# A block of attention and a bilinear FFN: order of the work in the opening and in the first block's attention

## Chip, cores and metric

The kernel runs on one core of a Trainium2 chip. The metric is the device time of one execution in microseconds (us). The kernel before was timed in three runs, 2474.35, 2477.37 and 2477.96 us, with a median of 2477.37.

## What is computed

The input is x, 2048 rows of 576 numbers. The block has two halves, each with a normalisation ahead of it and a sum with its input behind it:

```python
h  = x + A(layernorm(x))
h2 = h + B(layernorm(h))
# A: 32 query heads of 18, one key head and one value head for all of them
q = (x @ wq) in heads; k = x @ wk; v = x @ wv
p = softmax(q k^T * 18**-0.5);  A = concat(p v) @ wo
# B: 4608 hidden units, no nonlinearity
B = ((x @ w_gate) * (x @ w_up)) @ w_down
```

All is float32. Nearly every product is made of three passes: an operand is split into a high part (type fp32r) and the remainder, and high x high, high x low and low x high are added up.

## The kernel before

**Blocks, groups, pairs.** The rows are cut into four blocks of 512 queries. Attention of a block goes by eight groups of four heads; a group goes over 16 key tiles of 128 keys. One call of `pair` (L482) makes the scores of two heads against one key tile: two matmuls (`scores`, L500, the two heads side by side on rows 0 to 63 and 64 to 127 of the array) into a PSUM tile `s` of two banks, and one exponential on ACT (L503) from it to an SBUF tile `P`. Two pairs make a key tile of a group. There are 2 x 16 x 8 = 256 pairs in a block and 1024 in all. `s` has two buffers, so a third pair's scores wait until the first one's exponential has been read.

**Values.** `values` (L505) multiplies the four heads' exponentials of one key tile with V, four column strips side by side, into the accumulator `acc`, which has one PSUM bank. `flush(n)` (L510) issues the values of the n oldest key tiles in the list `pend`. After a group's last tile DVE copies `acc` to `os` (L518), and the output's transposition and division follow later as an "aux" (`normalise`, L532, and `normal_heads`, L540), then the transposition of finished chunks (L572); `run_aux(1)` runs at most one of these a step.

**The other PSUM banks.** Eight banks: four for `s`, two with the tag `f`, one `m` (bounds, transposes of outputs), one `a` (accumulator; in the opening the key projection `psk`).

**The opening, `keys_values` (L141 to L317).** Before any attention, the four blocks of x are loaded, normalised (`stats` on DVE, `scale` on DVE or POOL, `apply` on ACT), transposed on PE (`turn`), and split into high and low on ACT and DVE (`parts`); then keys and values of the block are projected on PE (`project`, 14 passes into `psk`), and brought into the form of `kT` by ACT, DVE and POOL (`keys`, whose second half is the function it returns). The query weights wq come by five loads of 128 x 576 and are split by `split_wq`: the high part on ACT, the low part on POOL. The first seven heads' queries of block 0 are projected here too (the 14 `next(first)` and the one behind them), sent to memory, and read back head by head (`load_q`). A bound of each query's scores needs the largest absolute keys of all four blocks: `kab`, `psb`, `G`, then `bounds(0)` and `load_m`. After that the first scores can start. The order of the calls is the order on every engine (`manual_schedule`): each engine takes its instructions in the order in which the program issues them, and SP's DMA queue does too.

**The first block's attention.** The loop in `run` (L840 to L849) makes block 0's attention while the queries of the 19 remaining (block, seven heads) tiles are projected: `queries` (L320) is a generator that yields after each pass, a pass being two matmuls of 64 rows into the two banks `psq` and `psr` (tag `f`). Behind the 14th pass it issues the eviction on DVE (L344 to L349), the DMAs to `q_dram`, and goes on to the next tile, whose first pass needs the same two banks. One step of the loop is four pairs; after each of them `due` grows by RATE = 1.25 and passes are issued while it is over zero, each of which takes 1 off. At the end of the step come one aux and `flush(len(self.pend) - 1)`: the values of all key tiles but the newest, two as a rule. When the generator is at its end, `steps` (L796) goes on in the same steps of four pairs without passes: to the end of the group, where a flag decides whether a bound was too loose (`guard`), and to the end of block 0's pairs, with the projections of the outputs and weights of the FFN put between. Then `fill` and the FFN (`ffn`) place the other blocks' pairs among their own matmuls.

Of the kernel before, what the change touches and what calls it, by code (L numbers as in the profile page):

```python
# [14 lines left out]
F32 = mybir.dt.float32  # L15
# [7 lines left out]
P = 128  # L23
# [32 lines left out]
class Block:  # L56
# [84 lines left out]
    def keys_values(self):  # L141
# [7 lines left out]
        xs = x01 + [x23[:, 0], x23[:, 1]]  # L149
        wqr = [(self.qp if c < 2 else self.qb).tile([P, D], F32, tag="q" if c < 2 else "qs", name=f"wqr{c}")  # L150
               for c in range(4)]
        for b in range(NB):
            for s in range(NQ):
                sp.dma_start(xs[b][:, s, :], self.x[b * TB + s * P: b * TB + (s + 1) * P, :])
            if b == 0:
                sp.dma_start(self.C, self.cst)
                sp.dma_start(wkv, self.wkv)
            if b == 1:
                for c in range(4):
                    sp.dma_start(wqr[c], self.wq[:, c, :])  # L160
        w_h = self.pp.tile([P, 5, P], F32R, tag="P", name="w_h")
# [60 lines left out]
        def project(b):  # L222
            psk = psks[b] = self.ps_a(f"psk{b}")
            for i, (w, m) in enumerate(passes(w_h, w_l, self.XT[b])):
                pe.matmul(psk, w, m, start=(i == 0), stop=(i == 13))
# [7 lines left out]
        def keys(b):  # L233

            sl = slice(b * TB, (b + 1) * TB)
            kk = self.pp.tile([P, 2, TB], F32R, tag="P", name=f"kk{b}")
            hi, k2 = kk[0:64, 0], f32(kk[0:64, 1])
            act.activation(hi, psks[b][0:64], AF.Identity, bias=nmean[0:64])
            dve.tensor_reduce(kabs[0:64, b:b + 1], f32(hi), AX.X, ALU.max, apply_absolute_value=True)

            def rest():
                if b:
                    dve.tensor_copy(kv[:, sl], psks[b])
                del psks[b]
                pool.tensor_scalar(k2, kv[0:64, sl], mb, nmb[0:64], ALU.mult, ALU.add)
                dve.scalar_tensor_tensor(self.kT[0:64, sl], f32(hi), ma, k2, ALU.mult, ALU.add)
                sp.dma_start(f32(self.kT[64:120, sl]), f32(self.kT[0:56, sl]))
            return rest

        first = self.queries(0)  # L250

        def split_wq(c):
            act.copy(self.wq_h[:, c], wqr[c])
            pool.tensor_tensor(self.wq_l[:, c], wqr[c], f32(self.wq_h[:, c]), ALU.subtract)

        act.copy(w_h, wkv)
        pool.tensor_tensor(w_l, wkv, f32(w_h), ALU.subtract)
        stats(0, 4)
        scale(0, 4, dve)
# [3 lines left out]
        scale(4, 8, pool)  # L263
        turn(0)
        stats(8, 12)
        scale(8, 12, pool)
        parts()
        split_wq(0)
        split_wq(1)
        apply(1)  # L270
        wqr.append(self.qp.tile([P, D], F32, tag="q", name="wqr4"))
        sp.dma_start(wqr[4], self.wq[:, 4, :])
        stats(12, 13)
        twice(dve)
        turn(1)
        stats(13, 16)
        scale(12, 16, pool)
        project(0)
        parts()
        apply(2)  # L280
        twice(dve)
        mean()
        turn(2)
        project(1)
        parts()
        keys(0)()
        split_wq(2)
        apply(3)
        twice(pool)
        late = keys(1)  # L290
        split_wq(3)
        split_wq(4)
        turn(3)
        late()
        project(2)
        parts()
        for _ in range(14):
            next(first)
        next(first)
        q = self.qt[0, 0] = self.qp.tile([P, 2, TB], F32R, tag="q", name="q0_0")  # L300
        self.load_q(q, 0, 0)
        keys(2)()
        project(3)
# [7 lines left out]
        self.load_m(q, 0, 0)  # L311
        late()
        psv = self.ps_a("psv")
        for t in range(NT):
# [5 lines left out]
    def queries(self, b):  # L320

        pe, act, dve, sp = self.pe, self.act, self.dve, self.sp
        for i, (h0, n) in enumerate(QT):
# [9 lines left out]
            else:  # L333

                psr = self.ps_f(f"psr{b}_{i}")
                for k, (w, m) in enumerate(passes(w_h, w_l, self.XT[b])):
                    for o, ps in ((0, psq), (64, psr)):
                        pe.matmul(ps[:r], w[o:o + 64], m[o:o + 64], start=(k == 0), stop=(k == 13))
                    yield 1
                    if k == 5 and self.tqs and self.tqs[0][0] < max(b, 1):  # L340
# [12 lines left out]
            self.tqs.append((b, h0, n, tq))  # L353
            if b == i == 0:
                yield 0
        if b == NB - 1:
            yield STEP
            yield STEP
            self.bounds(b)
# [436 lines left out]
    def steps(self, on):  # L796

        while on():
            for i in range(4):
                self.pair()  # L800
            self.run_aux(1)
            self.flush(len(self.pend) - 1)

    def run(self):
# [9 lines left out]
        with ExitStack() as st:  # L814
# [11 lines left out]
            with tc.tile_pool(name="p0q", bufs=1) as self.p0q:  # L826
# [3 lines left out]
                with tc.tile_pool(name="qb", bufs=2) as self.qb:  # L830
# [9 lines left out]
                    while live:  # L840
                        for i in range(4):
                            self.pair()
                            due += RATE
                            while due > 0 and live:
                                z = next(others, None)
                                live = z is not None
                                due -= z or 0
                        self.run_aux(1)
# [35 lines left out]

STEP = 2
RATE = 1.25
P_BUFS = 6
# [94 lines left out]
```

## Time and profile before

| What | Before |
|---|---|
| median of three runs | 2477.37 us |
| the profiled execution | 2473.66 us |
| its span, first to last instruction | 2471.9 us |
| first scores, PE L502 | 65.69 us |
| PE busy, share of the span | 2379.9 us, 96% |
| ACT busy | 1233.9 us, 50% |
| DVE busy | 1000.1 us, 40% |
| POOL busy | 356.4 us, 14% |
| exponentials, ACT L503 | 1024, 1027 ns each |

The profile is of one execution. Its page has the span in 40 slices, with the busy share of each engine as a digit (9 is 90% or more) and the clock granted to PE as a digit too. A row of the timeline gives the start in us, the length in us, the engine, the line, the operation, output and input, and how many instructions of that kind follow each other; in brackets stands how long the engine stood idle ahead of it and what ended that. A row of the waits gives who waited (engine, tile, line), for whom, the us in total, the number of times and the longest. A row of a group gives the instructions' count, their busy time and mean length in ns, and the idle time ahead of them. PEld is the loading of weights into PE. A matmul's length includes its way through the array, so that rows overlap; the time from start to start is what PE spends on it.

### The profile page before, as it was taken

What the parts mean: (1) busy time and instruction counts of PE and PEld (TensorE: products, weight loads), DVE (VectorE), ACT (ScalarE), POOL (GpSimd) and SP (SyncE); (2) the same over time, 40 slices, a digit from 0 to 9 for tenths busy, and PEclk for the clock granted to TensorE, in tenths of its full rate; (3) what the DMA queues carried; (4) which work ended last, traced back from release to release, by engine and by line L of the source; (5) the groups of instructions that cost most, each with busy time, mean ns of one, the idle gap of its engine ahead of it and who ended that gap; (6) DMA issues with size and microseconds to landing.
All of it is one profiled execution on the core that took longest, in us unless ns stands there. A gap on an engine that the chain in (4) does not pass through costs nothing. (4 is left out here: it accounts for less than half of the span.)

```text
span 2471.9 us, 44165 instructions
## 1 busy us (share of the span) xinstructions
PE 2379.9 (96%) x18833; PEld 1669.0 (68%) x18833; DVE 1000.1 (40%) x1719; ACT 1233.9 (50%) x1385; POOL 356.4 (14%) x402
## 2 busy tenths in 40 slices
PE   5888888999999999999999999999999999999999
PEld 4333333467776777776777767677767778888888
DVE  6322222433343334433333335343433364545544
ACT  5666665666556555466556564555565511111110
POOL 4000000011111111111111111111111112222221
PEclk8899997999999999999999999999999999999999
DMA  3211112222122221332212121241221122432221
GB/s 134 76 54 56 60 48 90 62 75 69 58 76 66 66 69 63 92 112 73 68 61 75 66 71 51 76 147 45 75 75 57 64 77 87 140 106 92 97 97 58
DMA packets 68706, 190.54 MB, mean 77 GB/s; under 512 B 7736, under 2 KB 7864, under 8 KB 68504
## 3 DMA queue, kind: packets, MB, share of 16 engines
q1 hardware_dynamic: 68504, 187.66, 23.8%
q8 instruction: 149, 2.44, 0.4%
q14 instruction: 53, 0.43, 0.1%
HBM read 159.39 MB, written 19.40 MB: 72 GB/s over the span
## 5 line engine op out<-in xcount | busy, mean ns | idle before, releaser
L503 ACT ACTIVATE P<-s 128x1024 f32<-128x1024 f32 x1024 | 1031.9, 1027 | 742.2 <-PE s L502 626.3
L743 PE MATMUL pg<-X,ws 64*128 64x512 f32 x2565 | 706.1, 392 | 0.0
L743 PE MATMUL pu<-X,ws 64*128 64x512 f32 x2565 | 705.6, 392 | 0.0
L743 PEld LDWEIGHTS pg<-X,ws 64*128 64x128 f32 x2565 | 474.4, 186 | 64.8 <-issue 6.1
L743 PEld LDWEIGHTS pu<-X,ws 64*128 64x128 f32 x2565 | 474.0, 186 | 40.0
L507 PE MATMUL acc<-P,V 128*32 128x512 f32 x4096 | 485.8, 605 | 5.8 <-DVE os L518 5.1
L502 PE MATMUL s<-q,kT 56*128 56x512 f32 x2048 | 442.6, 426 | 34.6 <-ACT P L503 28.2
L716 PE MATMUL y<-wds,ha 128*128 128x288 f32 x2304 | 464.1, 296 | 2.5 <-ACT ha L85 1.2
L716 PEld LDWEIGHTS y<-wds,ha 128*128 128x128 f32 x2304 | 368.4, 188 | 27.8 <-issue 25.2
L502 PEld LDWEIGHTS s<-q,kT 56*128 56x128 f32 x2048 | 196.4, 186 | 220.1 <-ACT P L503 108.6
L716 PE MATMUL y<-wds,hl 128*128 128x288 f32 x1152 | 340.1, 295 | 0.1
L743 PE MATMUL gu<-X,ws 64*128 64x512 f32 x2646 | 307.3, 389 | 0.0
L85 POOL CAST ws<-wr 128x1152 fp32r<-128x1152 f32 x144 | 166.3, 1155 | 970.0 <-PE pu L743 405.0
L507 PEld LDWEIGHTS acc<-P,V 128*32 128x32 f32 x4096 | 120.8, 110 | 273.1 <-issue 255.4
L743 PEld LDWEIGHTS gu<-X,ws 64*128 64x128 f32 x2646 | 247.8, 185 | 54.8 <-issue 4.2
L762 DVE TENSOR_TENSOR hf<-pu,g 128x512 f32<-128x512 f32 x95 | 65.7, 692 | 526.4 <-ACT g L758 526.4
L718 DVE TENSOR_TENSOR h<-h,y 128x288 f32<-128x288 f32 x384 | 172.8, 454 | 252.9 <-PE y L716 252.7
L758 ACT COPY g<-gu 128x512 f32<-128x512 f32 x49 | 28.8, 587 | 376.2 <-PE gu L743 376.2
L85 POOL CAST wds<-wdr 128x576 fp32r<-128x576 f32 x144 | 146.4, 1036 | 485.6 <-PE y L716 479.7
L716 PEld LDWEIGHTS y<-wds,hl 128*128 128x128 f32 x1152 | 216.1, 188 | 0.4 <-DVE hl L86 0.4
L86 DVE TENSOR_TENSOR ws<-wr,ws 128x1152 fp32r<-128x1152 f32 x144 | 204.5, 1420 | 0.0
L86 DVE TENSOR_TENSOR hl<-hf,ha 128x512 fp32r<-128x512 f32 x144 | 101.0, 702 | 152.6 <-ACT ha L85 152.6
(143 smaller groups left out, 1327.6 us busy)
## 6 DMA issues: line engine op xcount, KB each, us to landing
wr<-in_wgu_dram SPq DMA_DIRECT2D x144, 576.0 KB
wdr<-in_wd_dram SPq DMA_DIRECT2D x144, 288.0 KB
q<-q_dram SPq DMA_DIRECT2D x64, 216.0 KB
q_dram<-qs SPq DMA_DIRECT2D x16, 504.0 KB
X<-X SPq DMA_DIRECT2D x28, 256.0 KB
x<-in_x_dram SPq DMA_DIRECT2D x16, 288.0 KB
h<-in_x_dram SPq DMA_DIRECT2D x16, 288.0 KB
out_dram<-h SPq DMA_DIRECT2D x16, 288.0 KB
```

The lines of the kernel that those rows point to most:

```text
L85: (copy or self.cast)(hi, src)
L86: self.dve.tensor_tensor(lo, src, f32(hi), ALU.subtract)
L502: self.pe.matmul(s_[:, i], self.kT[o:o + 56, t * P:(t + 1) * P], q[o:o + 56, pr], start=True, stop=True)
L503: self.act.activation(p_, s_, AF.Exp, scale=SCALE)
L507: self.pe.matmul(acc[32 * j:32 * j + 32, :], self.V[:, t, :], Ps[j // 2][:, j % 2, :], start=(t == 0), stop=(t == NT - 1), skip_group_chec ...
L716: pe.matmul(y[:, :HD], m, w, start=(i == 0), stop=(i == len(ms) - 1))
L718: dve.tensor_tensor(hs, hs, y[:, :HD], ALU.add)
L743: pe.matmul(ps, w[o:o + 64, wk, c], X[o:o + 64, xk, c], start=(j == 0), stop=(j == 26))
L758: act.copy(g, pg)
L762: dve.tensor_tensor(hf, pu, g, ALU.mult)
```

## The change

It changes only order and sizes of work, not what is computed.

In the first attention a step has two pairs instead of four. RATE is 3.0 and is added once a step, after the first of the two pairs; passes follow there, the second pair follows without any. `flush(len(self.pend) - 1)` then issues one key tile's values. A tile's last pass takes 4 from `due` instead of 1, and `bounds(3)` at the end of the last block comes after one yield of 4 instead of two of 2. `steps` too has two pairs a step.

In the opening, the first seven heads' columns of wq come as one load of 128 x 5 x 126, behind the weights of keys and values and ahead of the second block's x; ACT and POOL split them directly after those weights. The other heads' columns come as one load of 128 x 5 x 450, issued behind the second block's keys, into the buffer that held the third and fourth block of x; POOL alone makes their high and low parts, tile by tile, at the end of the opening. `psk` uses the bank `a` for blocks 0 and 2 and a bank `f` for blocks 1 and 3. The tiles `kk` come from the ring of two buffers `qs` instead of the six of `P`. The first queries' passes stand ahead of the third block's normalisation, the projection of block 0 ahead of the second block's, and statistics, key steps and loads are ordered anew:

```diff
-        wqr = [(self.qp if c < 2 else self.qb).tile([P, D], F32, ...) for c in range(4)]
+        wqr = self.qp.tile([P, 5, 7 * DH], F32, tag="q", name="wqr0")
...
-            if b == 1:
-                for c in range(4):
-                    sp.dma_start(wqr[c], self.wq[:, c, :])
+                sp.dma_start(wqr, self.wq[:, :, 0:7 * DH])
...
-            psk = psks[b] = self.ps_a(f"psk{b}")
+            psk = psks[b] = (self.ps_f if b % 2 else self.ps_a)(f"psk{b}")
...
-            kk = self.pp.tile([P, 2, TB], F32R, tag="P", name=f"kk{b}")
+            kk = self.qb.tile([P, 2, TB], F32R, tag="qs", name=f"kk{b}")
...
+        w = (slice(None), slice(None), slice(0, 7 * DH))
+        act.copy(self.wq_h[w], wqr)
+        pool.tensor_tensor(self.wq_l[w], wqr, f32(self.wq_h[w]), ALU.subtract)
         stats(0, 4)
...
         turn(0)
+        parts()
         stats(8, 12)
         scale(8, 12, pool)
-        parts()
-        split_wq(0)
-        split_wq(1)
+        project(0)
         apply(1)
-        wqr.append(self.qp.tile([P, D], F32, tag="q", name="wqr4"))
-        sp.dma_start(wqr[4], self.wq[:, 4, :])
         stats(12, 13)
         twice(dve)
         turn(1)
-        stats(13, 16)
+        stats(13, 15)
+        for _ in range(14):
+            next(first)
+        parts()
+        stats(15, 16)
         scale(12, 16, pool)
-        project(0)
-        parts()
+        mean()
         apply(2)
         twice(dve)
-        mean()
         turn(2)
-        project(1)
-        parts()
-        keys(0)()
-        split_wq(2)
-        apply(3)
-        twice(pool)
-        late = keys(1)
-        split_wq(3)
-        split_wq(4)
-        turn(3)
-        late()
-        project(2)
-        parts()
-        for _ in range(14):
-            next(first)
         next(first)
         q = self.qt[0, 0] = self.qp.tile([P, 2, TB], F32R, tag="q", name="q0_0")
         self.load_q(q, 0, 0)
+        project(1)
+        parts()
+        late = keys(0)
+        apply(3)
+        twice(pool)
+        late()
+        turn(3)
+        project(2)
+        late = keys(1)
+        parts()
+        late()
+        wqr = self.otp.tile([P, 5, D - 7 * DH], F32, tag="oT", name="wqr1")
+        sp.dma_start(wqr, self.wq[:, :, 7 * DH:])
         keys(2)()
         project(3)
         late = keys(3)
...
         late()
+        for h0, n in QT[1:]:
+            w, o = (slice(None), slice(None), slice(h0 * DH, (h0 + n) * DH)), 7 * DH
+            pool.tensor_copy(self.wq_h[w], wqr[:, :, h0 * DH - o:(h0 + n) * DH - o])
+            pool.tensor_tensor(self.wq_l[w], wqr[:, :, h0 * DH - o:(h0 + n) * DH - o], f32(self.wq_h[w]), ALU.subtract)
...
-                    yield 1
+                    if k < 13:
+                        yield 1
...
-            if b == i == 0:
-                yield 0
+            yield 0 if b == i == 0 else 4
         if b == NB - 1:
-            yield STEP
-            yield STEP
+            yield 4
             self.bounds(b)
...
         while on():
-            for i in range(4):
-                self.pair()
+            self.pair()
+            self.pair()
             self.run_aux(1)
             self.flush(len(self.pend) - 1)
...
                     while live:
-                        for i in range(4):
-                            self.pair()
-                            due += RATE
-                            while due > 0 and live:
-                                z = next(others, None)
-                                live = z is not None
-                                due -= z or 0
+                        self.pair()
+                        due += RATE
+                        while due > 0 and live:
+                            z = next(others, None)
+                            live = z is not None
+                            due -= z or 0
+                        self.pair()
                         self.run_aux(1)
                         self.flush(len(self.pend) - 1)
...
-STEP = 2
-RATE = 1.25
+RATE = 3.0
```

More of the change, by code (lines that the diff above doesn't have):

```diff
@@ L149, in keys_values @@
         xs = x01 + [x23[:, 0], x23[:, 1]]
-        wqr = [(self.qp if c < 2 else self.qb).tile([P, D], F32, tag="q" if c < 2 else "qs", name=f"wqr{c}")
-               for c in range(4)]
+        wqr = self.qp.tile([P, 5, 7 * DH], F32, tag="q", name="wqr0")
         for b in range(NB):
@@ L250, in keys_values @@
         first = self.queries(0)
-        def split_wq(c):
-            act.copy(self.wq_h[:, c], wqr[c])
-            pool.tensor_tensor(self.wq_l[:, c], wqr[c], f32(self.wq_h[:, c]), ALU.subtract)
         act.copy(w_h, wkv)
         pool.tensor_tensor(w_l, wkv, f32(w_h), ALU.subtract)
+        w = (slice(None), slice(None), slice(0, 7 * DH))
+        act.copy(self.wq_h[w], wqr)
+        pool.tensor_tensor(self.wq_l[w], wqr, f32(self.wq_h[w]), ALU.subtract)
         stats(0, 4)
```

## The prediction

> **What bounds the kernel now.** The page first: span and slices. The profiled execution took 2473.66 us, its span 2471.9.
>
> ```profile
> span 2471.9 us, 44165 instructions
> PE   5888888999999999999999999999999999999999
> PEclk8899997999999999999999999999999999999999
> ```
>
> A slice is 61.8 us. From slice 7 on PE is hardly ever idle, and the change moves nothing after that slice: of 1024 pairs (a pair is two heads' scores against one key tile) the two kernels order all after the 278th alike. It touches slices 0 to 7; in 1 to 6 PE is eight tenths busy. The engine beside it there is ACT; the waits and its group from 75 to 345 us show both.
>
> ```profile
> ACT P L503 <- PE s L502: 89.4, 60, 4.1
> PEld s L502 <- ACT P L503: 76.1, 106, 0.9
> PEld acc L507 <- DVE os L518: 10.4, 6, 1.8
> PEld psq L338 <- DVE qs L344: 9.9, 14, 1.3
> PEld psr L338 <- DVE qs L345: 7.7, 14, 0.6
> L503 ACT ACTIVATE P<-s 128x1024 f32<-128x1024 f32 x189 | 179.8, 1028 | 89.4 <-PE s L502 89.4
> ```
>
> ACT is busy 179.8 of the 270 us. Neither engine is full, so they wait for each other: exponentials wait for scores (60 times, about once a step of four pairs), and scores wait for exponentials, because there are two score banks. One clean step in the timeline shows the loop:
>
> ```profile
> 151.08 0.50 PE L502 MATMUL s<-q,kT 56*128 56x512 f32 x2
> 151.69 3.77 ACT L503 ACTIVATE P<-s 128x1024 f32<-128x1024 f32 x4 [1.35 <-PE s L502]
> 151.88 0.40 PE L502 MATMUL s<-q,kT 56*128 56x512 f32 x2
> 152.11 0.40 PE L338 MATMUL psr<-XT,wq_h 64*126 64x512 f32 x1
> 152.76 0.50 PE L502 MATMUL s<-q,kT 56*128 56x512 f32 x2 [0.25 <-ACT P L503]
> 153.68 0.50 PE L502 MATMUL s<-q,kT 56*128 56x512 f32 x2 [0.19 <-ACT P L503]
> 154.34 1.92 PE L507 MATMUL acc<-P,V 128*32 128x512 f32 x16
> 156.20 0.50 PE L502 MATMUL s<-q,kT 56*128 56x512 f32 x2
> ```
>
> The step takes 156.20 - 151.08 = 5.12 us. ACT works 3.77 of it and then stands 1.35: PE puts both key tiles' values (1.86, from 154.34) in one block at the end, when ACT has only two scores in hand. Earlier in the step PE stands for a bank. A score or a query pass costs PE 0.23 (151.88 to 152.11).
>
> **The steps after the change.** A step is two pairs: a score, up to three passes, a score, one key tile's values. What one tile's block costs alone shows further on, in the fill before the FFN:
>
> ```profile
> 416.26 0.49 PE L502 MATMUL s<-q,kT 56*128 56x512 f32 x2
> 416.69 1.06 PE L507 MATMUL acc<-P,V 128*32 128x512 f32 x8
> 417.69 0.49 PE L502 MATMUL s<-q,kT 56*128 56x512 f32 x2
> 418.11 1.06 PE L507 MATMUL acc<-P,V 128*32 128x512 f32 x8
> ```
>
> From score to score 417.69 - 416.26 = 1.43: the score, the block, and two changes between them. It is dearer than half of a double block (1.00 against 0.93), and that is in the sum. A new step adds a score and n passes at 0.235 each: 2.37 for n = 3, 2.13 for 2, 1.90 for 1, 1.66 for 0. ACT needs 3.77/2 = 1.89 for two pairs, so a step is the larger of the two. It fits: an exponential starts 0.61 after its score (151.08 to 151.69) and its bank is free some 1.6 after it, before the same bank is asked for at 2.37; the values use the tile before, done 0.3 into the step. I see no wait in a clean step, and PE becomes the bound.
>
> The pull on the query generator: a step gives 3, a pass takes 1, and the last of a tile's 14 takes 4, so a tile takes 17. Three tiles go through 17 steps as 3 3 3 3 2, 1 3 3 3 3 1, 2 3 3 3 3 0: twelve of 2.37, two of 2.13, two of 1.90, one of 1.89, together 38.4 (42 passes). The 19 tiles left for this stage and the end of the last one make 110 steps (220 pairs, as before: 55 steps of four): six such rounds 230.4, then four of 2.37, one of 2.13 and three empty 17.3: **247.7 us**.
>
> Beside it on PE, moved but equal in number: the bounds' matmuls, transposes of the outputs and of the chunks.
>
> ```profile
> 354.68 0.66 PE L545 MATMUL pt<-C,os 128*128 128x128 f32 x4
> 373.22 1.36 PE L367 MATMUL psg<-tq,G 126*32 126x512 f32 x5
> ```
>
> Three groups of 1.36, four single ones at a fifth of that, nine transposes at 0.66: 11.1. The waits on DVE: at a tile's end the next pass now comes a score, a block and a score later, some 1.9 us after the last; DVE freed the second bank 1.9 after it before:
>
> ```profile
> 158.25 0.40 PE L338 MATMUL psr<-XT,wq_l 64*126 64x512 f32 x1
> 159.42 0.69 DVE L345 TENSOR_TENSOR qs<-psq,qs 126x512 f32<-126x512 f32 x1
> 160.16 0.50 PE L338 MATMUL psr<-XT,wq_h 64*126 64x512 f32 x1 [0.23 <-DVE qs L345]
> ```
>
> So it is met, just. The accumulator's bank likewise: a whole step now stands between one group's last block and the next group's first. Of the 28 us of such waits in the quoted rows I leave 4, for chunk transposes that follow the outputs' a step later, when DVE may be late, and 1.6 for the first step, whose PE work ran below full clock before and will again. Sum 264.4. Before:
>
> ```profile
> 65.69 1.01 PE L502 MATMUL s<-q,kT 56*128 56x512 f32 x2 [0.20 <-DMA q<-m_dram]
> 378.59 0.74 PE L502 MATMUL s<-q,kT 56*128 56x512 f32 x4
> ```
>
> 378.59 - 65.69 = 312.9 (pairs 1 to 220). **Gain 48.5.** Bounds: ACT alone would need 220 x 0.943 = 207, so not over 106; with every such wait kept (28 in 270 us, 32 in all), 28 more, a gain of 20.5.
>
> **The opening.** It ends with the key bound, which needs the last key projection. That one waited for its bank:
>
> ```profile
> 34.36 2.41 ACT L189 ACTIVATE xh<-x,n,ya 128x576 f32<-128x576 f32 x3
> ...
> 40.71 2.82 POOL L254 TENSOR_TENSOR wq_l<-wqr,wq_h 128x576 fp32r<-128x576 f32 x2 [2.44 <-ACT wq_h L253]
> 44.32 0.74 DVE L246 SCALAR_TENSOR_TENSOR kT<-kk,C 64x512 fp32r<-64x512 f32 x1 [2.82 <-POOL kk L245]
> 44.99 2.34 DVE L86 TENSOR_TENSOR XT<-tr,XT 128x1024 fp32r<-128x1024 f32 x2
> 47.36 0.69 DVE L95 TENSOR_TENSOR XT<-trt,XT 64x512 fp32r<-64x512 f32 x1
> 51.70 1.19 PE L225 MATMUL psk<-XT,w_h 128*128 128x512 f32 x2 [3.28 <-DVE kvw L243]
> 57.87 0.68 ACT L238 ACTIVATE kk<-psk,nmean 64x512 fp32r<-64x512 f32 x1 [8.25 <-PE psk L225]
> ```
>
> Its input was ready at 48.05 (47.36 + 0.69), it began at 51.70: with two banks 3.65 go. What then is late is DVE, which has the third tile's keys to copy first (one copy at 0.69): 0.7 back. DVE also stood 2.82 at L246, behind POOL's two weight splits; these leave, and the input is ready earlier.
>
> Against that stands the last tile's normalisation. Its statistics now come behind the second tile's splits on DVE (2.34 + 0.69 = 3.0), while POOL, which makes the scale of them, loses two weight splits ahead of it (2.82, priced as the two above). And the first weights' split has a price of its own:
>
> ```profile
> 9.46 1.53 POOL L257 TENSOR_TENSOR w_l<-kvw,w_h 128x640 fp32r<-128x640 f32 x1 [8.04 <-ACT w_h L256]
> 9.51 1.50 DVE L116 TENSOR_TENSOR ta<-ya 128x4 f32<-128x4 f32 x1
> ```
>
> A DVE instruction on four columns took 1.50 beside POOL's subtraction, to its end. A second subtraction, of 630 columns, now follows it beside the same chain: up to 1.5 later. The normalisation began at 34.36; it comes between 0 and 4.5 later, and stringing these durations queue by queue I get 2.7 (37.1). DVE's 2.82 less the part that this uses up leaves the input some 2 earlier. Last, the clock:
>
> ```profile
> 50.00:60.00 10.00, 6.42 (x16) 4.75 (x16) 3.15 (x7) 0.68 (x1) 0.77 (x1) 0.66 0.42 133
> ```
>
> The projection ran at a granted clock of 0.66 (the column before the DMA share), from 51.70 to just before 57.87, where 14 passes at 0.235 take 3.3. It began after 3.28 us of idle PE and will now follow the third one closely; I take 2 for it. Sum 3.65 - 0.7 + 2 + 2: **gain 7**, at least 1 (clock and POOL gains lost, the split late), at most 11. If the low clock came with the moment and not after idling, the gain is 5.
>
> The Trainium skill says in "TensorE: Matmul & The Clock Gate", section "Part 1: The HAM clock gate (the "warmup" mystery)", that an idle window of about 3.4 us halves the clock and a busy one restores it. By that rule the projection runs at full clock, as in my sum; the trace agrees in so far as 0.66 follows 3.28 us of idling.
>
> The strip of weights that ACT and POOL split before the first normalisation has rows of 126 x 4 = 504 bytes. The Trainium skill, "DMA: Bandwidth & Descriptors", section "Specifications", puts full rate at 512 bytes and more, with a read-modify-write below. By that page the strip is late. No row shows such a load; the nearest is the weights of keys and values, issued at 3.05 and used at 8.65:
>
> ```profile
> 3.05 0.43 SPq L157 DMA_DIRECT2D kvw<-in_wkv_dram  x1
> 8.65 0.73 ACT L256 CAST w_h<-kvw 128x640 fp32r<-128x640 f32 x1 [6.65 <-DMA kvw<-in_wkv_dram]
> ```
>
> At that rate the strip, issued at 3.5, lands by 9.5 and costs nothing; at twice the time it lands near 14.7, holds ACT's queue with the first normalisation behind it, and takes 1 to 2 us back. I take the first.
>
> POOL's eight splits of the other weights start when its last key step is done. The first piece must be there by the third pass: at most 1 us late. Their load, now a late one, stands in SP's queue behind the second tile's keys, some 6 us ahead of the bound's small DMAs.
>
> From pair 221 to 278 steps of two help only where outputs aren't projected: gain 1 (0 to 4; the flag's wait is untouched).
>
> **Sum**: 48.5 + 7 + 1 = 56.5, hence 2473.7 - 56.5 = 2417.2 for an execution like the profiled one. The median of the three runs shown, 2477.4, is 3.7 above it, so the median comes to 2420.9; I say **2420**.
>
> **Rivals.**
> 1. DVE's waits stay: a tile's five evictions, the bounds and the outputs share DVE, and "met, just" fails each time. For it: 0.2 us of margin. Against it: five at 0.69 or less are 3.5 of a tile's 13 us. 14 to 28 more: 2434 to 2448.
> 2. PE's parts pack better than the rows say and ACT's 207 us is the bound: 264.4 falls to some 225, 2381. Against it: the 1.43 stands in the rows.
> 3. The opening does not shorten: the strip late, the splits in the way, the clock low: 2427.
> 4. Slower. PE busier in the first attention lowers the clock it is granted there, as it did between 50 and 60 us. PE's 264 us turn into 400 at 0.66: 136 lost against 57 won, 2556. It decides at a mean of 264/321 = 0.82. Against it: the slices from 9 on have PE full at a clock of nine tenths and more.
>
> **How the numbers follow.** Forecast (gains 45 to 70, 2407 to 2432) 0.74; rival 1 0.12; rival 2 0.04; rival 3 0.07; rival 4 0.03. 2404 to 2440 takes in the forecast, the third and most of the first, and leaves out about 0.15. A measurement here tells 0.2%, 5 us, from no change: faster 0.96, same 0.01, slower 0.03.
>
> **What would show it.** ACT's idle, a third of the time from 75 to 345 us, falls to a fifth; exponentials come in twos, 2.4 apart; L338's waits for L344 and L345 nearly vanish; the first score stands near 58.7, the 221st pair's near 323; from the FFN on nothing differs but the start. It is wrong if passes or blocks cost more behind each other than in the rows quoted, or if a wait in each step, for a bank or for DVE, shows up instead.

## The result, and the profile after

The kernel after took 2412.61 us (median of four runs, 2410.95 to 2415.04), the kernel before 2475.86 (four runs, 2472.33 to 2477.96). The ratio is 0.9747, with a 95% interval of 0.973 to 0.9764. The forecast was 2420, the range 2404 to 2440. The profiled execution took 2414.04 us; before it was 2473.66, so 59.6 less, and 56.5 had been forecast. By the medians it is 63.3 less; the forecast of 2420 lay 57 below the median of three known then.

The page after, span, PE and PE's granted clock in 40 slices:

```profile
span 2412.3 us, 44160 instructions
...
PE   5999989999999999999999999999999999999999
...
PEclk9999999999999999999999999999999999999999
```

Slices 1 to 4 and 6 have gone from 8 to 9; the one 8 left, slice 5, holds the wait for the flag. To see where the 59.6 us came from, I cut each span at three rows of the timeline: the first score, the 221st pair, and the first transposition for the FFN (`tx`). The first two rows of the kernel after:

```profile
59.65 1.07 PE L498 MATMUL s<-q,kT 56*128 56x512 f32 x2 [1.48 <-DMA q<-m_dram]
...
325.07 0.73 PE L498 MATMUL s<-q,kT 56*128 56x512 f32 x4
```

| Stage (us) | Before | After | Gain | Forecast |
|---|---|---|---|---|
| opening, to the first score | 65.7 | 59.65 | 6.0 | 7 |
| pairs 1 to 220 | 312.9 | 265.4 | 47.5 | 48.5 |
| 221st pair to `tx` (472.84, 412.23) | 94.3 | 87.2 | 7.1 | 1 |
| from `tx` to the end | 1999.1 | 2000.1 | -1.0 | 0 |

**The first attention.** The waits of the kernel after between 70 and 312 us (who waited, for whom, us in total, times, longest), and its group of exponentials from the same stretch:

```profile
PEld s L498 <- ACT P L499: 77.7, 95, 0.9
ACT P L499 <- PE s L498: 45.4, 92, 2.3
```

```profile
L499 ACT ACTIVATE P<-s 128x1024 f32<-128x1024 f32 x202 | 196.8, 1024 | 46.0 <-PE s L498 45.4
```

ACT stands 46.0 of 242 us, a fifth instead of a third, and now about once in two exponentials, 0.5 us at a time. Waits on DVE for the query banks are gone from PE. The 77.7 us in the first row are no loss: it is the weight load that stands there, ahead of its turn. What the matmuls themselves waited for, from 80 to 300 us, is four rows before and two after:

```profile
PE s L502 <- ACT P L503: 13.5, 57, 0.5
PE acc L507 <- DVE os L518: 4.2, 5, 0.9
PE psq L338 <- DVE qs L344: 4.0, 6, 0.8
PE psr L338 <- DVE qs L345: 2.9, 12, 0.3
```

```profile
PE to L134 <- DVE ob L550: 2.0, 1, 2.0
PE acc L503 <- DVE os L514: 2.0, 1, 2.0
```

One clean step in the timeline, from score to score 69.65 - 67.30 = 2.35 us, with nothing in brackets on PE:

```profile
67.30 0.50 PE L498 MATMUL s<-q,kT 56*128 56x512 f32 x2
...
67.90 1.95 ACT L499 ACTIVATE P<-s 128x1024 f32<-128x1024 f32 x2 [0.47 <-PE s L498]
...
68.33 0.39 PE L498 MATMUL s<-q,kT 56*128 56x512 f32 x2
68.66 1.06 PE L503 MATMUL acc<-P,V 128*32 128x512 f32 x8
69.65 0.50 PE L498 MATMUL s<-q,kT 56*128 56x512 f32 x2
```

**The opening** of the kernel after, in the rows that answer to those of the prediction:

```profile
8.96 1.51 DVE L117 TENSOR_TENSOR ta<-ta,va 128x4 f32<-128x4 f32 x1
9.09 0.72 ACT L252 CAST wq_h<-wqr 128x630 fp32r<-128x630 f32 x1 [0.25 <-DMA wqr<-in_wq_dram]
10.41 1.43 POOL L253 TENSOR_TENSOR wq_l<-wqr,wq_h 128x630 fp32r<-128x630 f32 x1
10.51 1.35 DVE L122 SCALAR_TENSOR_TENSOR ya<-ta,yia 128x4 f32<-128x4 f32 x1
...
12.09 0.16 DVE L117 TENSOR_TENSOR ta<-ta,va 128x4 f32<-128x4 f32 x1
...
38.31 3.14 ACT L186 ACTIVATE xh<-x,n,ya 128x576 f32<-128x576 f32 x4 [1.73 <-POOL n L178]
...
46.33 0.50 PE L222 MATMUL psk<-XT,w_h 128*128 128x512 f32 x1 [0.23 <-DVE XT L86]
...
49.72 0.68 ACT L235 ACTIVATE kk<-psk,nmean 64x512 fp32r<-64x512 f32 x1 [3.08 <-PE psk L222]
...
51.53 0.74 DVE L243 SCALAR_TENSOR_TENSOR kT<-kk,C 64x512 fp32r<-64x512 f32 x1 [0.97 <-POOL kk L242]
52.20 0.67 DVE L236 TENSOR_REDUCE kabs<-kk 64x1 f32<-64x512 f32 x1
```

The last key projection waits for no bank: it starts at 46.33 (51.70 before), as soon as the first pieces of its input are there, and is done in 3.39 us (6.17 before). Then DVE keeps the fourth tile's keys waiting: ready at 50.40, they are taken up at 52.20. Before, DVE took them up 0.72 after ACT began on them (57.87):

```profile
58.59 0.68 DVE L239 TENSOR_REDUCE kabs<-kk 64x1 f32<-64x512 f32 x1 [5.39 <-ACT kk L238]
```

### The profile page after: what moved, and what is told of

Read it like the earlier page. It is cut to its first block, busy times and chain, and to the rows that moved or that the text cites. A ratio compares the mean times of both kernels' runs of the same rounds, so it can differ in the third digit from the quotient of the medians.

```text
span 2412.3 us, 44160 instructions
## 1 busy us (share of the span) xinstructions
PE 2357.6 (98%) x18833; PEld 1658.7 (69%) x18833; DVE 999.1 (41%) x1719; ACT 1235.2 (51%) x1381; POOL 357.9 (15%) x406
## 4 chain that ended last, share of the span: by engine, by line
PE 95%; DVE 2%; ACT 1%; issue 1%; DMA 1%; POOL 0%; SPq 0%; ACTq 0%; POOLq 0%; DVEq 0%
PE acc L503 19%; PE y L712 19%; PE pg L739 14%; PE gu L739 12%; PE s L498 12%; PE pu L739 11%; PE yo L608 3%; PE psq L335 2%; PE pt L541 1%; ACT P L499 1%; PE to L134 0%; PE tx L657 0%; DVE bsa L100 0%; PE psr L335 0%; DVE XT L86 0%
## 5 line engine op out<-in xcount | busy, mean ns | idle before, releaser
L503 PE MATMUL acc<-P,V 128*32 128x512 f32 x4096 | 491.2, 599 | 2.6 <-DVE os L514 2.0
L498 PE MATMUL s<-q,kT 56*128 56x512 f32 x2048 | 434.0, 421 | 12.9 <-DVEq L388 8.0
L503 PEld LDWEIGHTS acc<-P,V 128*32 128x32 f32 x4096 | 114.4, 109 | 250.4 <-issue 225.1
L758 DVE TENSOR_TENSOR hf<-pu,g 128x512 f32<-128x512 f32 x95 | 65.7, 691 | 528.6 <-ACT g L754 528.6
```

Source lines behind the costliest of these rows:

```text
L498: self.pe.matmul(s_[:, i], self.kT[o:o + 56, t * P:(t + 1) * P], q[o:o + 56, pr], start=True, stop=True)
L503: self.pe.matmul(acc[32 * j:32 * j + 32, :], self.V[:, t, :], Ps[j // 2][:, j % 2, :], start=(t == 0), stop=(t == NT - 1), skip_group_chec ...
L758: dve.tensor_tensor(hf, pu, g, ALU.mult)
```

## The experiments

Times are medians. Where a ratio to the kernel before stands beside one, it has its 95% interval; one with no ratio is a single run. Stages are cut as above, in the one execution of each kernel that was profiled.

| Kernel | Time | First score | Pairs 1 to 220 | To `tx` | After `tx` |
|---|---|---|---|---|---|
| loop_only | 2417.68 | 64.9 | 264.6 | 87.4 | 1996.9 |
| opening_only | 2465.79 | 59.9 | 313.0 | 91.1 | 1999.1 |
| values_by_two | 2440.23 | 59.4 | 293.4 | 87.2 | 1998.0 |
| double_score | 2435.53 | 58.7 | 287.8 | 87.2 | 2000.0 |
| short_exp | 2449.25 | 66.0 | 287.3 | 93.8 | 2000.4 |
| steps_four | 2421.16 | 59.6 | 265.0 | 91.7 | 1998.9 |
| one_bank | 2422.0 | 69.4 | 264.6 | 87.3 | 1999.0 |
| split_later | 2411.03 | 57.8 | 265.0 | 87.1 | 1997.2 |
| keys_behind | 2411.22 | 55.8 | 266.3 | 87.0 | 2000.4 |

In values_only and no_off the flag comes at another pair, so for those two only the sum of the two middle stages compares.

### The two halves of the change

loop_only is the kernel before with the loop, `steps` and the generator's yields of the kernel after. opening_only is the kernel after with those taken from before:

```diff
-                        self.pair()
-                        due += RATE
+                        for i in range(4):
+                            self.pair()
+                            due += RATE
...
-RATE = 3.0
+STEP = 2
+RATE = 1.25
```

> The opening of the kernel before with the loop and the later steps of the changed one. Stages of the profiles so far: first score at 65.69 us before and 59.65 after; 220 pairs from there in 312.9 and 265.4; from the 221st pair to the transposes ahead of the FFN 94.3 and 87.2. If the stages don't act on each other, this kernel has 65.7, 265 and 87: 6 us more than the changed kernel, about 2419. Rival: the low clock of the opening's end is carried into the loop and the loop needs the new opening for its gain: 270 or more in the second stage.

> The opening of the changed kernel with the loop and the later steps of the one before. If the stages don't act on each other: first score at 59.7, then 313, then 94: 6 us less than the kernel before, about 2470. Rival: part of the loop's gain comes from the opening (weights at hand, a warmer clock): under 308 in the second stage.

loop_only took 2417.68 us, 0.9765 (0.9749 to 0.9782), opening_only 2465.79, 0.9957 (0.9941 to 0.9974). In the first two stages the halves add up: the loop alone turns 312.9 us into 264.6, the opening alone 65.7 into 59.9, and neither moves the other's stage by a microsecond. So the loop's gain isn't the opening's, and nearly nine tenths of what these two stages gain (47.5 of 53.5) belong to it. The whole times do not add up as well: by the medians of their session the halves gain 59.6 and 11.5 us, together 71.1 where both gave 63.3, and opening_only came out 4 us below the 2470 expected. Some 3 of that is the stage up to `tx`, where opening_only gained 3.2 with the order of the kernel before; why is not shown.

### What in the loop makes it faster

values_only keeps values at each key tile, but places the passes as before, one or two behind each pair, with no step off at a tile's end. values_by_two keeps steps of two and three passes, but issues values every other step, for two key tiles. no_off lets a tile's last pass take 1 from `due`, so that the next tile's first pass may follow at once. Their edits, in this order and cut to the lines that matter:

```diff
-                        self.pair()
-                        due += RATE
-                        while due > 0 and live:
...
-                        self.pair()
+                        for i in range(2):
+                            self.pair()
+                            due += RATE
+                            while due > 0 and live:
```

```diff
-                        self.flush(len(self.pend) - 1)
+                        if self.n_pair % 4 == 0:
+                            self.flush(len(self.pend) - 1)
```

```diff
-                    if k < 13:
-                        yield 1
+                    yield 1
...
-            yield 0 if b == i == 0 else 4
+            if b == i == 0:
+                yield 0
```

> The changed kernel, but query passes are issued as before: RATE 1.25 after each of the two pairs, no step off at a tile's end. Values stay at each key tile. My theory of the prediction (values at each tile take PE and ACT apart, PE becomes the bound): second stage 265 plus the waits for DVE at tiles' ends, 10 to 25, so 275 to 290. Rival, that three passes between a step's scores make the gain: 295 or more.

> The changed kernel with the values of two key tiles every second step; passes stay at three a step with a step off. My theory of the prediction taken strictly (the double block of values is what starves ACT) says that much of the gain goes: second stage 285 or more. The rival worked out by rows: a score, three passes, a score twice, then the double block is 1.04 + 0.24 + a wait of 0.4 for the bank + 1.04 + 0.33 + 1.86 = 4.9 for four pairs, against 4.74 in the changed kernel: only 5 to 10 us more, 270 to 276, since the three passes between the scores already hide the exponentials.

> The changed kernel, but a tile's last pass takes 1 like the others, so that the next tile's first pass may follow it in the same step. If the step off is what removed the waits for DVE's evictions: they come back in two tiles of three, some 1.7 us each, and 3 us for more steps without passes: second stage 285 to 290 instead of 265. Rival, that PE has other work to do by then in any case: 265 to 270.

values_only took 2427.44 us, 0.9799 (0.9783 to 0.9815); its two middle stages take 368.3 us against 352.6 of the kernel after, 15.7 more. values_by_two took 2440.23, 0.9854 (0.9838 to 0.9871), and its first 220 pairs 28.0 more. no_off took 2432.99, 0.9832 (0.9807 to 0.9857), and its two middle stages 373.5, 20.9 more. So values at each key tile give most: with the new opening and `steps` of two (worth 4.5 here by steps_four below), but without the new placing of the passes, the two middle stages go from the 407.1 of the kernel before to 368.3. Three passes a step on top of them lose 5.2 if no step is put off at a tile's end, and gain 15.7 if one is: those two belong together.

What the double block does is seen in a step of values_by_two:

```profile
149.90 3.79 ACT L499 ACTIVATE P<-s 128x1024 f32<-128x1024 f32 x4 [2.30 <-PE s L498]
...
150.98 0.49 PE L498 MATMUL s<-q,kT 56*128 56x512 f32 x2 [0.24 <-ACT P L499]
...
152.93 1.92 PE L503 MATMUL acc<-P,V 128*32 128x512 f32 x16
...
154.78 0.50 PE L498 MATMUL s<-q,kT 56*128 56x512 f32 x2
...
155.38 3.92 ACT L499 ACTIVATE P<-s 128x1024 f32<-128x1024 f32 x4 [1.69 <-PE s L498]
```

The exponentials again come in fours. ACT ends its fourth at 153.69, in the middle of the block of 1.92 us, and stands until the first score behind the block is there; earlier in the step PE stands for ACT (0.24 at 150.98). An output's four transposes, from 152.34 to 152.93, also stand ahead of this block and lengthen the wait. But for them, this is the step that the kernel before had. PE's own instructions cost no more so (a double block costs less than two single ones): most of the 28 us are idle PE. In 220 us, from 80 to 300, PE was busy 197.13 us there, and 216.03 in the kernel after. Its matmuls waited 16.3 us for ACT there (none in the kernel after) and 6.1 for DVE at the accumulator (2.0 in the kernel after). Some 3 of the 28 are clock, as an estimate: 0.54 was granted from 190 to 200 us and 0.75 in the next 2, which costs 5.1, against 1.7 in the kernel after (0.83, 0.50 and 0.82 in windows of 2 us from 140).

In no_off, PE waits for DVE, from 70 to 340 us:

```profile
PE psq L335 <- DVE qs L341: 9.6, 12, 0.9
...
PE psr L335 <- DVE qs L342: 2.7, 12, 0.3
```

12.3 us are these waits. Without the step off, the passes are also used up sooner, after 182 pairs, and 19 of the 110 steps have none, which cost ACT's 1.89 each. As an estimate from the prediction's rows, 91 x 2.37 + 19 x 1.89 = 251.6 is 3.9 over the 247.7 of the kernel after. That leaves 4.7 of the 20.9 that these rows do not settle. It is more when one counts that the kernel after has 4.0 of other waits on DVE, nearly all of which no_off lacks, and that PE's stand at the flag is 8.0 there and 4.1 here.

### Which engine bounds the steps, new and old

double_score writes the second pair's scores twice in each step of the loop; nothing else follows from it. short_exp is the kernel before with exponentials of half the length: it leaves out the second head's in the first 220 pairs.

```diff
+        if self.twice:
+            for i, o in enumerate((0, 64)):
+                self.pe.matmul(s_[:, i], self.kT[o:o + 56, t * P:(t + 1) * P], q[o:o + 56, pr], start=True, stop=True)
         self.act.activation(p_, s_, AF.Exp, scale=SCALE)
```

```diff
-        self.act.activation(p_, s_, AF.Exp, scale=SCALE)
+        if self.short:
+            self.act.activation(p_[:, 0], s_[:, 0], AF.Exp, scale=SCALE)
...
+            i = 0 if id(Ps[j // 2]) in self.halves else j % 2
```

> The changed kernel with the second pair's two score matmuls of each step issued twice into the same bank (the second overwrites the first with the same numbers). If PE bounds the new steps, 0.235 in each of 110 steps is added, less in the steps without passes: second stage 22 to 26 us longer, 287 to 291. If ACT or the score banks bound them, 0 to 8.

> The kernel before, in which the exponentials of the first 220 pairs take one head's 512 columns instead of two heads' 1024; both heads' values are made from that one. This leaves out half of these pairs' exponentials and keeps every instruction of PE and DVE. Theory (the old step of four pairs loses its time because one block of both key tiles' values outlasts the two score tiles that ACT has in hand, after which PE in turn waits for a score tile): with exponentials of some 0.6 us instead of 0.94, ACT has spare time in every step, PE no longer waits for it, and the 312.9 us of the first 220 pairs fall to PE's own work, 240 of steps (247.7 less 55 x 0.14 for double blocks) + 11.1 + 1.6, plus most of the up to 32 of waits on DVE: 265 to 285. The 221st pair then stands at 331 to 351, and the time is 2425 to 2447. Rival (the old steps are long for reasons other than ACT: the waits on DVE and PE's own order): 300 us or more, time 2460 or more.

double_score took 2435.53 us, and its first 220 pairs 22.4 us more: 0.204 for each of the 110 scores added. Added PE work goes into the time nearly whole, as it should where PE bounds the steps, and rival 2 (ACT as the bound) falls. A score bank that came free too late could have shown the same, since the second writing also delays the exponential; against that stand PE's rows of the kernel after, which have no wait for ACT from 80 to 300 us.

short_exp took 2449.25, and its first 220 pairs 287.3 us, 25.6 less than the kernel before and just over the 265 to 285 expected. Its exponentials, between 75 and 345 us:

```profile
L504 ACT ACTIVATE P<-s 128x512 f32<-128x512 f32 x206 | 120.3, 598 | 150.3 <-PE s L502 142.7
```

With ACT idle more than half the time, the old steps win back what they lost to ACT: 25.6 of the 47.5. What PE's matmuls still wait for in it, from 75 to 345 us, is DVE alone:

```profile
PE psq L338 <- DVE qs L344: 7.8, 15, 0.8
PE acc L512 <- DVE os L523: 5.0, 6, 0.9
PE psr L338 <- DVE qs L345: 3.4, 14, 0.3
```

In the same stretch of the kernel before, PE's rows have 17.2 us of waits for ACT and 12.4 for DVE. A wait costs more than its row says, since it is counted from the end of a matmul's way through the array: in the old step that the prediction shows, 152.76 - 152.11 = 0.65 with 0.25 marked, where a pass costs 0.23, so 0.17 is lost beside the 0.25. As an estimate, the 35 waits of 16.2 us in short_exp come to 22 so. The other 21.9 of the 47.5 are near that, and near what the placing of the passes is worth (15.7 by values_only, 20.9 by no_off). So somewhat over half of the loop's gain is the two engines' alternate waiting, and the rest is, as far as these rows tell, mostly the waits on DVE. It is not a full account: the single blocks of the new steps are dearer by 55 x 0.14 = 7.7, which the kernel after pays and short_exp does not.

### The stage behind the loop

steps_four is the kernel after with `steps` in steps of four:

```diff
         while on():
-            self.pair()
-            self.pair()
+            for i in range(4):
+                self.pair()
```

> The changed kernel with four pairs a step behind the query passes again (pairs 221 to 256). The third stage, 94.3 us before and 87.2 after, had its clock low for 50 us before and for 20 after. If the short steps shorten it, it goes back to 92 or more here, 5 to 7 us lost. Rival: the clock came back earlier by chance of its moment and the steps are worth 1 us at most: 86 to 89.

It took 2421.16 us, 0.9785 (0.9761 to 0.981), and 91.7 us from the 221st pair to `tx` instead of 87.2, just under the 92 expected: steps of two are worth 4.5 there, where I had put 1. That is one trace, of the fastest of its four runs (2417.06); by the medians the steps are worth 8.5. In this stage PE's scores waited 7.3 us for ACT before, 7.7 in steps_four and 2.4 after. Another part is a short loss of clock, seen in the kernel before in windows of 2 us (busy time of PE, PEld, DVE, ACT and POOL, then PE's granted clock):

```profile
420.00:422.00 2.00, 0.80 (x4) 0.37 (x4) 0.00 (x0) 2.00 (x3) 0.00 (x0) 1.00 0.00 0
422.00:424.00 2.00, 2.00 (x11) 1.88 (x10) 0.85 (x2) 1.48 (x2) 0.00 (x0) 0.65 0.00 0
424.00:426.00 2.00, 2.00 (x11) 1.14 (x13) 0.96 (x3) 0.00 (x0) 0.00 (x0) 0.50 0.00 0
426.00:428.00 2.00, 2.00 (x18) 0.43 (x10) 0.00 (x0) 1.02 (x1) 0.00 (x0) 1.00 0.00 0
```

Four scores stand one behind the other ahead of that, the next two have to wait for ACT (PE busy 0.80 of 2 us), and then PE runs at half clock for about 3.4 us: 0.35 x 2 + 0.5 x 2 = 1.7 us lost. steps_four has the same place, four scores at 362.59 and waits of 0.93 and 0.42 for ACT behind them, and the same loss in its window of 10 us; the kernel after, whose steps have two scores and one block, does not have it:

```profile
360.00:370.00 10.00, 8.65 (x50) 4.47 (x52) 2.12 (x5) 5.82 (x6) 0.00 (x0) 0.83 0.01 2
```

```profile
360.00:370.00 10.00, 10.00 (x72) 5.35 (x74) 3.34 (x8) 6.83 (x7) 0.00 (x0) 1.00 0.01 2
```

The other 2.6 of the 7.1 are not the change's doing that I can show: opening_only has the order of the kernel before in this stage and took 91.1, 3.2 less than it. Where they lie is seen behind the flag's wait, in windows of the kernel before and of the kernel after:

```profile
390.00:400.00 10.00, 7.03 (x24) 2.48 (x24) 0.00 (x0) 6.16 (x7) 1.15 (x1) 0.50 0.53 197
```

```profile
340.00:350.00 10.00, 8.99 (x44) 3.02 (x44) 1.08 (x6) 7.18 (x8) 1.15 (x1) 0.69 0.37 140
```

Before, PE worked for some 20 us behind the wait at a low clock (0.50 from 390 to 400, 0.67 from 400 to 410), after for some 10 us at 0.69. PE's stand at the flag itself was longer after, 8.0 us against 5.2. Why the clock came back earlier was not tried.

### The opening

one_bank is the kernel after with one bank for the key projections:

```diff
-            psk = psks[b] = (self.ps_f if b % 2 else self.ps_a)(f"psk{b}")
+            psk = psks[b] = self.ps_a(f"psk{b}")
```

> The changed kernel with all four key projections in the bank a. If the second bank is worth what the prediction says, the last projection waits for the copy of the third one's keys and the first score comes about 3 us later, 62.5. Rival: DVE's queue ahead of the last keys hides the wait, and the first score stays within 1 us of 59.65.

It took 2422.0 us, and the first score came at 69.41, 9.8 later than in the kernel after and 3.7 later than before the change, where 62.5 had been expected. Not one projection waits for the bank but two, the third and the fourth:

```profile
46.92 0.69 DVE L240 COPY kvw<-psk 128x512 f32<-128x512 f32 x1
...
47.76 1.19 PE L222 MATMUL psk<-XT,w_h 128*128 128x512 f32 x2 [3.90 <-DVE kvw L240]
...
56.28 0.70 PE L222 MATMUL psk<-XT,w_h 128*128 128x512 f32 x2 [2.23 <-DVE kvw L240]
```

In the new order the second tile's copy that frees the bank (46.92) stands behind the fourth tile's splits on DVE. The third projection then also ran slow: 6.39 us from 47.76 to the start of ACT on it at 54.15, against 3.59 in the kernel after. So the new order needs the second bank: together they gain 6, the order alone would lose.

split_later moves POOL's subtraction for the first heads' weights behind the second tile's scale. keys_behind does that too, and moves the third tile's key step behind the bound; its tile `kk` then comes from the ring `P`, and `keys` gives back the copy and the rest as two functions. The main lines:

```diff
-        pool.tensor_tensor(self.wq_l[w], wqr, f32(self.wq_h[w]), ALU.subtract)
         stats(0, 4)
...
         scale(4, 8, pool)
+        pool.tensor_tensor(self.wq_l[w], wqr, f32(self.wq_h[w]), ALU.subtract)
```

```diff
-        keys(2)()
+        late2 = keys(2)
         project(3)
...
         self.load_m(q, 0, 0)
-        late()
+        late2[0]()
+        late[0]()
+        late2[1]()
+        late[1]()
```

> The kernel after, with POOL's subtraction for the first heads' weights moved from ahead of the first normalisation to behind POOL's scale of the second tile. If the 1.35 us by which DVE's statistics lag beside that subtraction reach the end of the opening, the first score comes 1 to 1.4 earlier (58.3 to 58.7, after: 59.65) and the time is 2410.5 to 2412. If they are taken up by waits further on, or POOL is late at its new place, the first score stays at 59.4 to 60.5 and the time within 2 us of the kernel after's.

> split_later, and the third tile's copy, POOL step and kT step (L240, L242, L243) moved from ahead of the fourth tile's largest absolute keys to behind the loading of the bound; the copies of both tiles come first there. The prediction took 0.7 us for what stands on DVE ahead of the fourth tile's keys. If the whole key step stands there, DVE's wait for POOL in its middle included, the fourth tile's largest keys, 2.48 after the last projection's end in the kernel after, come 0.7 after it, as in the kernel before, and the first score stands 1.8 earlier than in split_later: 55.9 to 56.4. Rival (0.7, the copy alone, is what goes, or V, which is now made later, holds the first values): first score at 57.1 or later, or the 221st pair less than 1 us earlier than in split_later. The time is 2407 to 2410 by the first and 2410 to 2412 by the second.

split_later: 2411.03 us, 0.9743 (0.973 to 0.9757). The first normalisation starts at 11.85 instead of 13.47, the last at 36.47 instead of 38.31, and the first score stands at 57.81, 1.8 earlier: the split's price had gone through the whole opening, a little more than expected. keys_behind: 2411.22 us, 0.9738 (0.9725 to 0.9752). Its fourth tile's keys and first scores:

```profile
47.69 0.68 ACT L236 ACTIVATE kk<-psk,nmean 64x512 fp32r<-64x512 f32 x1 [3.02 <-PE psk L222]
...
48.41 0.68 DVE L237 TENSOR_REDUCE kabs<-kk 64x1 f32<-64x512 f32 x1 [0.41 <-ACT kk L236]
...
55.81 1.09 PE L506 MATMUL s<-q,kT 56*128 56x512 f32 x2 [0.30 <-DMA q<-m_dram]
...
58.22 0.79 PE L343 MATMUL psq<-XT,wq_l 64*126 64x512 f32 x1 [0.47 <-POOL wq_l L317]
```

The keys are taken up 0.72 after ACT began on them, and the first score comes another 2.0 earlier, as the first theory said. But the 221st pair comes only 0.7 earlier than in split_later (322.07 against 322.77), which was the rival's sign. Its reason is not borne out: V is there at 57.27 and the first values start at 61.50. What the rows show is that the first passes now wait for POOL's split (0.47), and that PE runs at half clock until about 63 us in both kernels (0.50 from 56 to 60, then 0.54 in split_later and 0.58 here from 60 to 64), so that scores which start sooner run slow for longer; no run separates the two. Both kernels' times are 1 to 2 us under the kernel after's, and their ranges overlap with its range: they are no proven gain.

## Why the prediction was right

Its sum, 56.5, came out at 59.6 in the profiled executions, and its reason holds: two halves of the step that waited for each other, and DVE at a tile's end. That the sum is so near owes something to luck: the stages are off by -1.0, -1.0, +6.1 and -1.0. Step by step:

- **Steps of the loop: 48.5 forecast, 47.5 measured.** The clean step was put at 2.37 and takes 2.35; the 4 us left for waits on DVE are the 4.0 in the rows above, though only half of them are the chunk transposes that I left them for; the other 2.0 are a wait for the accumulator's bank, which I took to be met. The 28 us of waits on DVE before, and with them the lower bound of 20.5, were read from rows of PEld; in PE's own rows they are 12.4. PE as the bound is shown by double_score, the cause of the old waits by values_by_two and short_exp, the waits on DVE by no_off and short_exp. The margin that I called "met, just" held, and rival 1 did not come.
- **The opening: 7 forecast, 6.0 measured**, with errors both ways. Bank and earlier input: 3.65 + 2 forecast, 5.37 measured (51.70 - 46.33). The last piece of the input was only 1.06 earlier (46.30 + 0.69 = 46.99), not 2, but the projection did not wait for it and began 0.66 ahead. Clock: 2 forecast, 2.78 measured (6.17 - 3.39). DVE behind the projection: 0.7 forecast, 1.76 measured (2.48 - 0.72). This is the mis-sized term: I counted one copy, but the whole key step of the third tile stands there, DVE's wait for POOL (0.97) in its middle. keys_behind shows it. Another 0.35 was lost from there to the first score.
- **The split beside the statistics.** "Up to 1.5 later" was real: the second subtraction made an instruction that otherwise takes 0.16 last 1.35, beside the first one's 1.51, which was there before (1.50). split_later shows that all of it reached the first score. The last normalisation was put at 37.1 and came at 38.31. The Trainium skill, "SBUF — State Buffer", section "Who interferes with whom", says that a DVE instruction with two SBUF inputs contends with a GpSimd instruction that reads SBUF. These two rows, 1.51 and 1.35, each with two inputs beside POOL's subtraction, agree.
- **The strip of 504-byte rows.** It came at no cost: used at 9.09, when 9.5 was the forecast. The Trainium skill, "DMA: Bandwidth & Descriptors", section "Specifications", has a read-modify-write below 512 bytes. The prediction's estimate for a load of twice the time was 14.7; the 9.09 shows no such price here.
- **The clock of the last projection.** It came back with the idling gone, as the sum had it: 1.00 was granted from 46 to 50 us. By the Trainium skill's page "TensorE: Matmul & The Clock Gate", section "Part 1: The HAM clock gate (the "warmup" mystery)", an idle window of about 3.4 us costs the full clock and no such window stands ahead of it now; the 3.39 us for 14 passes agree. In other places much shorter stands halved the clock too (last section).
- **Pairs 221 to 278: 1 forecast, 0 to 4 as bounds, 7.1 measured.** This term was mis-sized, and its bounds too narrow. The step of four costs 4.5 there, since I had counted only the waits in the steps without projections and not the clock that such a wait takes with it. The rest, 2.6, is not traced to the change: the kernel before and opening_only, with the same order in this stage, differ by 3.2. The flag's wait, called untouched, grew from 5.2 to 8.0.
- **Rival 4, the clock lowered by a busier PE:** 0.99 granted in the loop before and after. Nothing speaks for it.

## What to carry to other kernels

With two buffers between a producer and a consumer, the longest block that the producer does for something else must be shorter than what the consumer has in hand; cut such a block even if the pieces cost more in sum (here 1.00 against 0.93), and look for two engines that wait for each other in turn. Where a step's last item needs buffers that another engine empties, put other work between, about as long as the emptying. A term that is "one instruction on the way" should be counted to the end of the queue that is issued ahead of the instruction that matters, its waits on other engines included.

## What the runs showed of the hardware

PE's clock was halved without PE having stood still for long. In the kernel before, from 420 to 422 us, PE was busy 0.80 of 2 us, its longest stand 0.93; from about 422.6 to 426.0 it then ran at 0.50. The same followed on such a stretch in short_exp, here in windows of 2 us, where PE's two marked stands are 0.82 and 0.79 us (for DVE, up to 195.29 and 197.80):

```profile
194.00:196.00 2.00, 1.18 (x16) 0.16 (x8) 0.69 (x1) 0.00 (x0) 0.00 (x0) 1.00 0.00 0
196.00:198.00 2.00, 1.21 (x9) 0.45 (x5) 0.91 (x2) 0.60 (x1) 0.00 (x0) 0.95 0.00 0
198.00:200.00 2.00, 2.00 (x9) 1.29 (x10) 1.93 (x4) 0.17 (x1) 0.00 (x0) 0.50 0.00 0
```

A wait of a microsecond in an else busy stretch may thus cost another 1.7 us or more, and a change that takes such waits away gains more than the waits. The length of one stand does not decide it alone: of the two stands of 2.0 us in the kernel after, the one that ended at 140.39 was followed by a stretch at 0.50, the one that ended at 224.15 was not (1.00 granted from 220 to 230). No kernel was made to find out how much idling it takes.
